# Attention and router kernel: the ranks of the tokens as two products of 16-bit whole numbers, 25 expert tiles without a branch, and one branch over all that remains

## The chip, the core and the metric

The kernel runs on one core of a Trainium2 chip. The metric is the time of one execution in microseconds of the device. The core has five engines that work side by side, each with its own queue of instructions: PE (TensorE, matrix products; the profile lists its loading of weights as PEld), DVE (VectorE), ACT (ScalarE), POOL (GpSimd, which here also issues the indirect DMAs) and SP (SyncE, which issues the other DMAs). They wait for each other with semaphores.

## What is computed

The reference has two parts. The first is attention with a block mask, for 4 batches, 8 heads, 768 positions and 64 values a head:

```python
scores = scale * np.matmul(q, k.transpose(0, 1, 3, 2))
scores = np.where(mask, scores, -1000000000.0)
attn = np.exp(scores - np.max(scores, axis=-1, keepdims=True))
attn = attn / (np.sum(attn, axis=-1, keepdims=True) + 1e-09)
attn_out = np.matmul(attn, v)
```

Its output, laid out as 3072 tokens of 512 values, goes to 8 experts. Each token takes one expert, the one whose embedding is nearest to it by cosine:

```python
logits = xn @ en.T / tau
expert_idx = np.argmax(logits, axis=1)
gate_w = probs[np.arange(N), expert_idx]      # softmax of the logits
for e in range(E):
    mask = expert_idx == e
    h = np.maximum(x[mask] @ w1[e], 0.0)      # 512 -> 1024
    out[mask] = gate_w[mask, None] * (h @ w2[e])   # 1024 -> 512
```

## The kernel before

**Attention** (`attention_fast`, up to about 320 us) runs over 16 pairs of heads. Each pair has 12 units of work: 128 keys against 384 queries, for two heads in 64x64 quarters of PE. For each unit PE makes the scores (L368), ACT the exponentials (L371), DVE adds up the denominators (L385, L387), and PE multiplies by v (L390). This path takes no maximum first; if a denominator comes out of bounds, a slow exact path (`exact`) has to compute everything again. `count_good` (L467 and after) counts the denominators that are in bounds into `good`.

**Routing** (`route`) follows each batch of 768 tokens: it makes the one-hot choice of each token, `oh`, on DVE (L541), and on POOL the running count `seen` of tokens by expert, one column of 128 tokens after another (L545, six small additions). **Ranks** (`rank`, L563 and after) then give each token its place among those with the same expert. Within a column of 128 tokens the number before a token is a product of a triangular matrix, `before`, with `oh` (L569). The number in earlier columns is a product of a matrix of ones with `seen` (L570), added up in the same place in PSUM. A third product with ones gives the totals by expert (L571), which DVE copies into `count` (L573). All are 32-bit. `rank` runs once a batch: three times amid attention, at a fixed unit of the plan in `after_sequence`, and the fourth time after the first expert tile, in `between` of `fast`.

**Experts.** Tokens are sorted by expert into tiles of 128. The first 5 tiles (`NE`) are made from the first two batches, while attention goes on; their places are computed by `dispatch_early`. All other tokens go into at least 19 late tiles (`NU`), because 24 x 128 = 3072, and at most 24 (`NL`), because an expert's last tile can be partly empty. How many are used is known on the device only, in `used` (L743), which `dispatch_late` computes on DVE. Two of the late tiles are mixed: they hold two experts, in halves of 64 tokens.

`expert_tiles` (L1087) runs the tiles. Each of them does the following.

- `fetch` (L850) issues on POOL the gathers of the rows of the tile after the next (L817, four indirect DMAs), and on SP the loads of the weights of up to three tiles ahead (L846, two loads of 2 MB for each expert).
- `expert_tile` (L886) makes the first layer on PE (L896, 64 products), takes its positive part on ACT (L899) and DVE (L903), and prepares the next tile's rows on DVE (L877 to L882). Then it makes the second layer (L911, 8 products of 512 columns, two passes each).
- `finish` multiplies by the gate on DVE (L919) and scatters the rows to the output by an indirect DMA on POOL (L920).

The first 24 tiles run always. The others stand in nested branches: the 25th runs if `used` is above 19, the 26th if it is above 20, and so on. Each branch is an instruction on each engine (L1105), which needs `used` in a register (L1104, a load). At the end of such a block each engine waits until all that was issued in it is done. The program is then at the last branch (L1204 and L1205), over the whole exact path, taken if `good` is not the full count. The instructions of the exact path stand between that branch and the end of the program.

The order of the instructions on an engine is that of the code, except where `issue_after` sets another; routing steps and ranks are put between units of attention by the plan in `after_sequence`.

## Time and profile before

Four runs took 698.47 to 699.81 us, with a median of 699.05. The profiled execution is another one:

| | us |
|---|---|
| profiled execution, time | 698.63 |
| profiled execution, span from the first to the last instruction | 696.8 |
| PE busy with matmuls | 682.0 |
| DVE busy | 344.9 |
| POOL busy | 296.4 |
| ACT busy | 188.4 |
| last matmul of PE ends at about | 683.9 |
| scatter of the last tile is issued by POOL at | 685.0 |

The profile's page gives the busy time of each engine, and the span in 40 equal slices, with the busy share of each engine in tenths and the clock that PE was granted. Other views list the waits of an engine with what ended them, the instructions of one line, or a stretch of time in order. In a row such as `L569 PE MATMUL rk<-oh,before` the line of the code comes first, then the engine, the operation and the names of the output and the inputs; `x8` is a count. An engine name with a q (POOLq) marks instructions that the engine's sequencer handles alone: branches, loads of registers, waits. PE's matmuls overlap, so a matmul's own duration is longer than the distance to the next one's start; distances between starts tell what PE needs for a piece of work.

### The profile page before, as it was taken

How to read it: one execution, taken by the hardware profiler on the slowest of the kernel's cores; microseconds unless marked ns; L12 is line 12 of the kernel's file. 1: busy time of each engine (PE TensorE's matmuls, PEld its weight loads, DVE VectorE, ACT ScalarE, POOL GpSimd, SP SyncE). 2: the span in 40 equal slices, each digit the busy share in tenths (PEclk: the TensorE clock that was granted, in tenths of full speed). 3: DMA queues.
4: the chain of work that ended last, by engine and by line, in shares of the span. 5: the costliest groups of instructions: out<-in, count | busy, mean ns of one | idle time of the engine just before them, and what ended most of it. 6: DMA issues, size and time to landing. Idle time of an engine off the chain costs nothing.

```text
span 696.8 us, 19415 instructions
## 1 busy us (share of the span) xinstructions
PE 682.0 (98%) x8237; PEld 452.9 (65%) x8237; DVE 344.9 (49%) x733; ACT 188.4 (27%) x266; POOL 296.4 (43%) x450
## 2 busy tenths in 40 slices
PE   9999999999999999999999999999999999999992
PEld 4777777555555557557767677666576755667770
DVE  6887778877788888765771111211112111211120
ACT  5455555555555455453100000000100000000000
POOL 1355466544774468545402244224332343323430
PEclk9999999999999999999999999999999999999997
DMA  7832344575326669653999889999899998999990
GB/s 122 132 68 51 47 70 71 130 155 108 59 42 155 141 160 210 218 162 106 330 407 375 324 313 343 341 348 320 305 409 403 406 370 310 420 391 418 353 346 25
DMA packets 172650, 164.87 MB, mean 237 GB/s; under 512 B 129340, under 2 KB 129340, under 8 KB 169478
## 3 DMA queue, kind: packets, MB, share of 16 engines
q1 hardware_dynamic: 165734, 149.86, 68.0%
q0 software_dynamic: 5216, 13.43, 5.2%
q8 instruction: 68, 1.11, 0.7%
q10 hardware_dynamic: 1600, 0.20, 0.2%
q14 instruction: 32, 0.26, 0.1%
HBM read 147.66 MB, written 16.07 MB: 235 GB/s over the span
## 4 chain that ended last, share of the span: by engine, by line
PE 96%; DMA 1%; issue 1%; POOL 0%; DVE 0%; ACT 0%; POOLq 0%
PE hp L896 23%; PE sc L368 22%; PE yp L911 22%; PE av L390 18%; PE back L425 3%; PE hp L939 2%; PE yp L959 2%; PE back L418 2%; DMA out_dram<-y,slot_l 1%; PE warm L81 1%; PE hp L951 0%; PE xg_ps L872 0%; PE rk L569 0%; POOL out_dram L920 0%; POOL xg L817 0%
## 5 line engine op out<-in xcount | busy, mean ns | idle before, releaser
L371 ACT ACTIVATE e<-sc 128x768 f32<-128x768 f32 x192 | 155.5, 810 | 149.1 <-PE sc L368 147.8
L896 PEld LDWEIGHTS hp<-xgt,w 128*128 128x128 f32 x1472 | 167.8, 192 | 10.8 <-issue 10.2
L896 PE MATMUL hp<-xgt,w 128*128 128x128 f32 x1472 | 169.3, 275 | 0.0
L368 PE MATMUL sc<-qt,kt 64*64 64x384 f32 x1536 | 163.5, 482 | 0.0
L911 PE MATMUL yp<-w,h 128*128 128x512 f32 x368 | 161.7, 592 | 0.0
L390 PE MATMUL av<-e,vld 64*64 64x384 f32 x1536 | 159.7, 486 | 0.0
L387 DVE TENSOR_TENSOR esum<-esum,e 128x768 f32<-128x768 f32 x128 | 129.2, 1010 | 34.2 <-ACT e L371 30.3
L911 PEld LDWEIGHTS yp<-w,h 128*128 128x128 f32 x368 | 68.2, 190 | 77.0 <-issue 76.0
L453 POOL TENSOR_TENSOR sq<-sq 128x192 f32<-128x192 f32 (+1 forms) x186 | 103.4, 556 | 13.9
L817 POOL DMA_INDIRECT xg<-x_dram,quarter x88 | 88.3, 1003 | 32.9 <-issue 27.7
L390 PEld LDWEIGHTS av<-e,vld 64*64 64x64 f32 x1536 | 63.7, 133 | 46.1 <-issue 17.3
L899 ACT ACTIVATE h<-hp 128x512 f32<-128x512 f32 x23 | 13.7, 597 | 291.4 <-PE hp L896 264.6
L903 DVE TENSOR_SCALAR h<-hp 128x512 f32<-128x512 f32 x23 | 15.9, 692 | 149.7 <-PE hp L896 146.3
L920 POOL DMA_INDIRECT out_dram<-y,slot_l x20 | 20.1, 1007 | 156.4 <-DVE y L919 151.1
L368 PEld LDWEIGHTS sc<-qt,kt 64*64 64x64 f32 x1536 | 66.2, 133 | 31.5 <-issue 22.8
L449 POOL TENSOR_TENSOR sq<-x 128x384 f32<-128x384 f32 x31 | 28.4, 917 | 115.6 <-DVE part L438 97.6
L368 PE MATMUL sc<-qmask,kmask 64*64 64x384 bf16 x768 | 72.6, 323 | 0.1
L919 DVE TENSOR_SCALAR y<-yp,gate 128x512 f32<-128x512 f32 x20 | 15.0, 751 | 81.0 <-PE yp L911 68.8
L368 PEld LDWEIGHTS <-kmask 64*64 64x64 bf16 x768 | 31.3, 107 | 26.4 <-issue 21.3
L385 DVE TENSOR_TENSOR esum<-e 128x768 f32<-128x768 f32 x32 | 31.2, 976 | 7.2 <-ACT e L371 7.1
L425 PE MATMUL back<-ones,esum 64*64 64x1 f32 x1536 | 27.5, 190 | 0.0
L425 PEld LDWEIGHTS back<-ones,esum 64*64 64x64 f32 x1536 | 26.6, 135 | 0.0
(204 smaller groups left out, 365.9 us busy)
## 6 DMA issues: line engine op xcount, KB each, us to landing
w<-in_moe_w_dram SPq DMA_DIRECT2D x54, 2048.0 KB
w<-in_moe_w_dram SPq DMA_DIRECT2D x16, 512.0 KB
x_dram<-x SPq DMA_DIRECT2D x24, 258.0 KB
vld<-in_v_dram SPq DMA_DIRECT2D x32, 192.0 KB
kld<-in_k_dram SPq DMA_DIRECT2D x60, 96.0 KB
qld<-in_q_dram SPq DMA_DIRECT2D x60, 96.0 KB
x_early<-x SPq DMA_DIRECT2D x12, 258.0 KB
xg<-x_dram,quarter POOLq DMA_INDIRECT x88
```

The costliest lines, as they stand in the source:

```text
L368: nc.tensor.matmul(ps[D * r:D * (r + 1), h, 0:HALF], lhsT=rows[D * h:D * (h + 1), keys], rhs=cols[D * h:D * (h + 1), queries], start=first ...
L371: k.exps = nc.scalar.activation(e, ps[:, :, 0:HALF], ACT.Exp, scale=SCALE)
L385: k.summed = nc.vector.tensor_tensor(out=k.esum, in0=k.first, in1=e, op=ALU.add)
L387: k.summed = nc.vector.tensor_tensor(out=k.esum, in0=k.esum, in1=e, op=ALU.add)
L390: nc.tensor.matmul(k.av[D * h:D * (h + 1), r, 0:HALF], lhsT=v[D * r:D * (r + 1), h, kc, :], rhs=e[D * r:D * (r + 1), h, :], start=(kc == 0 ...
L425: nc.tensor.matmul(sums[D * s:D * (s + 1), t, h, r:r + 1], lhsT=esum[D * r:D * (r + 1), h, cols], rhs=k.ones[D * r:D * (r + 1), 0:1], star ...
L449: nc.gpsimd.tensor_tensor(out=sq, in0=x, in1=x, op=ALU.mult)
L453: k.squared = nc.gpsimd.tensor_tensor(out=out, in0=sq[:, :, 0:width], in1=sq[:, :, width:2 * width], op=ALU.add).ins
L817: k.nc.gpsimd.indirect_dma_start(out=x[:, g], out_offset=None, in_=quarters, in_offset=bass.IndirectOffsetOnAxis(ap=k.quarter[:, g, t:t + ...
L896: nc.tensor.matmul(hp[:, f, :], lhsT=w1[:, d, (f0 + f) * P:(f0 + f + 1) * P], rhs=xt[:, d, :], start=(d == 0), stop=(d == ND - 1))
L911: nc.tensor.matmul(yp, lhsT=h[:, f, :], rhs=w2[:, f, :], start=(f == 0), stop=(f == NF - 1))
L920: k.scattered = nc.gpsimd.indirect_dma_start(out=k.out[:, :], out_offset=bass.IndirectOffsetOnAxis(ap=slot, axis=0), in_=y[:, :], in_offse ...
```

## The change

The ranks. `oh`, `seen`, the triangular matrix and a second matrix of ones become 16-bit (bf16, in which whole numbers up to 256 are exact). The product with ones now spans the seven columns of `seen` at once, the six for the ranks and the one for the totals, and comes first; the product with `before` is added to six of them. So two products take the place of three.

The tiles. `FULL = min(NU + 1, NL)` is 20. The 5 + 20 = 25 tiles always run, in one loop, and `fetch` and `prepare` look no further than the last of them (`k.stop`). Before, they looked ahead to all 29 tiles that there could be.

The branch. `count_good` also computes `todo`: one if a denominator was out of bounds, plus one if `used` is above 20. A single branch on `todo` stands behind the loop. In it, `more` runs the tiles from the 26th on, in nested branches on `used` as before, but with their own buffers and without any loads ahead, and then the branch on `good` with the exact path.

```diff
+FULL = min(NU + 1, NL)
...
-    k.before = pool.tile([P, P], F32, name="before")
+    k.ones_b = pool.tile([P, P], BF16, name="ones_b")
+    nc.vector.memset(k.ones_b, 1.0)
+    k.before = pool.tile([P, P], BF16, name="before")
...
-    k.oh = pool.tile([P, NT, E], F32, name="oh")
+    k.oh = pool.tile([P, NT, E], BF16, name="oh")
     k.rank = pool.tile([P, NT], F32, name="rank")
-    k.seen = pool.tile([P, NT + 1, E], F32, name="seen")
+    k.seen = pool.tile([P, NT + 1, E], BF16, name="seen")
...
+    bad = k.dp.tile([P, 1], F32, name="bad")
+    nc.vector.tensor_scalar(out=bad, in0=ps[:, 0:1], scalar1=float(N * H), scalar2=None, op0=ALU.is_lt)
+    tiles = k.dp.tile([P, 1], F32, name="tiles")
+    nc.vector.tensor_scalar(out=tiles, in0=k.used, scalar1=float(FULL), scalar2=None, op0=ALU.is_gt)
+    k.todo = k.const.tile([P, 1], I32, name="todo")
+    nc.vector.tensor_tensor(out=k.todo, in0=bad, in1=tiles, op=ALU.add)
...
-    nc.tensor.matmul(rk, lhsT=k.before, rhs=oh, start=True, stop=False)
-    nc.tensor.matmul(rk, lhsT=k.ones, rhs=k.seen[:, b * NC:(b + 1) * NC, :], start=False, stop=True)
-    nc.tensor.matmul(ps[:, NC * E:(NC + 1) * E], lhsT=k.ones, rhs=k.seen[:, (b + 1) * NC, :], start=True, stop=True)
+
+    nc.tensor.matmul(ps[:, 0:(NC + 1) * E].rearrange("p (c e) -> p c e", e=E), lhsT=k.ones_b,
+                     rhs=k.seen[:, b * NC:(b + 1) * NC + 1, :], start=True, stop=False)
+    nc.tensor.matmul(rk, lhsT=k.before, rhs=oh, start=False, stop=True)
...
-    if i + 2 < NE + NL and i + 2 != NE:
+    if i + 2 < k.stop and i + 2 != NE:
         fetch_rows(k, i + 2)
-    need = [(t, at) for t in range(NE + NL) for at in parts(t)]
+    need = [(t, at) for t in range(k.stop) for at in parts(t)]
...
-    if i + 1 < NE + NL:
+    if i + 1 < k.stop:
         prepare(k, i + 1)
...
-    between, n.scattered = iter(between), None
-    for i in range(NE + NU):
+    between, n.scattered, n.stop = iter(between), None, NE + FULL
+    for i in range(NE + FULL):
...
+def last_tiles(n):
+
     used = n.nc.values_load(n.used[0:1, 0:1], min_val=0, max_val=NL)
     with ExitStack() as more:
-        for i in range(NU, NL):
+        for i in range(FULL, NL):
             more.enter_context(n.tc.If(used > i))
-            n.scattered = None
-            fetch(n, NE + i)
+            n.scattered = n.relu = None
+            n.stop = NE + i + 1
+            fetch_rows(n, NE + i)
+            for at in parts(NE + i):
+                for _ in fetch_weights(n, NE + i, at):
+                    pass
+            prepare(n, NE + i)
             expert_tile(n, NE + i)
...
+def more(n):
+
+    n.rings, n.loads = {}, 0
+    with ExitStack() as ctx:
+        def pool(name, bufs, **kw):
+            return ctx.enter_context(n.tc.tile_pool(name=name, bufs=bufs, **kw))
+
+        n.wp, n.wp2 = pool("wp_l", 1), pool("wp2_l", 1)
+        n.eps, n.hps = pool("eps_l", 1, space=PSUM), pool("hps_l", 1, space=PSUM)
+        last_tiles(n)
+    good = n.nc.values_load(n.good[0:1, 0:1], min_val=0, max_val=N * H)
+    with n.tc.If(good < N * H):
+        exact(n)
...
     fast(n)
-    good = n.nc.values_load(n.good[0:1, 0:1], min_val=0, max_val=N * H)
-    with tc.If(good < N * H):
-        exact(n)
+    todo = n.nc.values_load(n.todo[0:1, 0:1], min_val=0, max_val=2)
+    with tc.If(todo > 0):
+        more(n)
```

## The prediction

> **What bounds the kernel.** I read the page's first two parts, then the list of waits of TensorE (PE), then the stretches in which the change works, in order of time.

> ```profile
> span 696.8 us, 19415 instructions
> ...
> PE 682.0 (98%) x8237; PEld 452.9 (65%) x8237; DVE 344.9 (49%) x733; ACT 188.4 (27%) x266; POOL 296.4 (43%) x450
> ...
> PEclk9999999999999999999999999999999999999997
> ```

> ```profile
> PE warm L81 <- DVE zeros L78: 1.3, 1, 1.3
> PE hp L951 <- issue: 0.5, 2, 0.2
> ```

> PE is busy for 98% of the span at the full granted clock, and these two rows are all the waits that it has. No load of weights, gather or eviction holds it anywhere. So a microsecond taken out of PE's own work is a microsecond of the end, wherever it stands; the other part of the span to be had is the tail, from PE's last matmul (about 683.9 us) to 696.8 us: 12.9 us in which no engine computes for long. The change touches both.

> **The ranks.** They run four times: at 118.9, 198.2 and 278.1 us amid attention and at 340.1 us between the first two expert tiles. The timeline of PE shows the first and the last of them (start, busy us, line), and the nearest thing to what replaces them, a product with 16-bit weights of 128x128 and 10 columns, also amid attention:

> ```profile
> 118.95 0.42 PE L569 MATMUL rk<-oh,before 128*128 128x48 f32 x2
> 119.20 0.39 PE L570 MATMUL rk<-seen,ones 128*128 128x48 f32 x2
> 119.43 0.35 PE L571 MATMUL rk<-seen,ones 128*128 128x8 f32 x2
> 119.71 0.88 PE L390 MATMUL av<-e,vld 64*64 64x384 f32 x8
> ```

> ```profile
> 257.91 0.46 PE L658 MATMUL slot_ps<-val,lanes 128*128 128x10 bf16 x12
> 258.30 0.88 PE L390 MATMUL av<-e,vld 64*64 64x384 f32 x8
> ```

> ```profile
> 340.14 0.32 PE L569 MATMUL rk<-oh,before 128*128 128x48 f32 x2
> 340.30 0.39 PE L570 MATMUL rk<-seen,ones 128*128 128x48 f32 x2
> 340.52 0.35 PE L571 MATMUL rk<-seen,ones 128*128 128x8 f32 x2
> 340.73 1.47 PE L896 MATMUL hp<-xgt,w 128*128 128x128 f32 x11
> ```

> Each 32-bit product is two passes of weights and matmul, so a rank is six passes. From its first to the next work: 119.71 - 118.95 = 0.76 us in attention, 340.73 - 340.14 = 0.59 us among the tiles. The twelve 16-bit passes take 258.30 - 257.91 = 0.39 us, and their starts in the trace lie 26 ns apart, so two of them take 0.39 - 10 x 0.026 = 0.13 us, the switch back to the 64x64 matmuls included. Among the tiles the same line (24 passes at 369.71, the next matmul at 370.32) costs 25 ns a pass, two 0.05 us. The gain is 3 x (0.76 - 0.13) + (0.59 - 0.05) = 1.9 + 0.5 = **2.4 us**. Bounds: if each 16-bit product cost as much as a 32-bit one, one product of three goes, 0.22 us four times, 0.9 us; if the 0.08 us more that the first and third rank wait before they start went too, 2.6 us. I take 2.4, by the nearest row, which has the same weights, type and neighbours.

> What stands around it: the product with the counts now comes first, so PE waits for GpSimd's adds (L545) 0.2 us sooner. At the first rank they end at 112.94 + 2.93 = 115.87 us, 3.1 us ahead; at the last at 340.07 us, 0.07 us before PE is free. I cost this at 0 to 0.1 us. VectorE gets a fill of the 16-bit ones and three tiny operations (0.16 us each by their neighbours, 0.5 in all). The nearest matmul to need VectorE behind them is the fifth yp of the first tile after the rank, due at 348.39 + 4 x 0.43 = 350.1 us; its half of h is ready at 348.85. The 1.2 us between hide it, so nothing; without that cover it would be 0.5 us. New waits of PE on itself (the first `back` after a rank, the first slot_ps) are for matmuls a score group or more earlier, and cost nothing; draining PE there, 0.5 us by the length of one sc matmul, four times 2 us, would be the other end, and stays inside the range.

> **The 25th tile.** Line 920 scatters 5 + 20 tiles, so the 25th tile runs in this data already, behind the branch. PE has no gap at that branch (14.0 us between the starts of tiles, as before it), because its sequencer runs ahead: PE's own branch row stands at 665.8 us, the matmuls behind it start at 669.7. So running it always saves nothing in PE. Four weight loads of 2 MB (SP, at 650 to 670 us) and eight gathers of 1.0 us on GpSimd, made for tiles 26 and 27, go; nothing waits for them, and they cost nothing either way.

> **The tail.** Here the branches matter. Rows of the branch lines, with the times of first and last start:

> ```profile
> L1104 POOLq TENSOR_LOAD <-used x1: 516/516/516, 670.7 to 670.7; - x1
> ```

> ```profile
> L1105 POOLq EVENT_SEMAPHORE  x4: 17/43/43, 685.0 to 688.6; - x4
> ```

> ```profile
> L1205 POOLq EVENT_SEMAPHORE  x6: 17/30/43, 692.3 to 692.8; - x6
> ...
> L1205 POOLq COMPARE_BRANCH  x1: 50/50/50, 689.6 to 689.6; - x1
> L1205 POOLq INC_SWDGE_SEM  x1: 410/410/410, 694.5 to 694.5; - x1
> ```

> The last y ends at 684.71 us. GpSimd issues its scatter (684.99 to 686.00), waits at the join of the inner branches until it has landed (688.4), releases its queue (688.7, 0.42), loads `good` (689.3, 0.30) and branches over the fallback at 689.6. Its next instruction starts at 692.3, 2.7 us later; in between only instruction packets move. VectorE shows the same at its own jump (685.4 to 688.3). Then come waits to 692.8, 1.7 us with nothing, the queue's release at 694.5, a drain, and the end.

> After the change there is one branch and no join ahead of it. GpSimd loads `todo` as soon as the last scatter is handed over. The load of `used` shows when that is: y of the tile before ended at 670.70, the load began at 670.7, beside the scatter (670.98), and the branch ran at 671.3. So: y ends 684.71, branch 685.3, jump 2.7, first instruction behind it at 688.0 instead of 692.3. The scatter lands at 688.4 meanwhile, when the waits reach it. From there to the end all stays: **4.3 us** less. PE and VectorE jump no later than today and are done by 689.0, so GpSimd still ends last. Bounds: 0.7 us, if the load is held until the scatter has landed (3.6 us later than I take it); 5.9 us, if the idle 1.7 us before the release goes as well. I take 4.3, from the same engine's own load and jump.

> [...]

> **The sum.** 2.4 + 4.3 = 6.7 us. The profiled execution took 698.63 us (span 696.8), so 691.9 by it; the median of the four runs, 699.05, lies 0.4 above, so **692.3 us**.

> **Rivals.**
> - *The second pause goes too* (0.20). The 1.7 us before the last release look like a second piece of code that is fetched because the jump lands near the end of the first. The new code lies elsewhere. SP shows such a second pause (677.6 to 681.4), VectorE and ACT, which have less left to run, do not. 2.4 + 5.9 = 8.3 us: 690.8.
> - *The jump is not moved forward* (0.10). GpSimd's load of `todo` waits for the scatter, or the fetch takes as long as SP's (671.5 to 677.6, 6.1 us). For it: the old join did wait for the landing. Against it: the load of `used` did not. 2.4 + 0.7 = 3.1: 696.0.
> - *Slower* (0.04): GpSimd's adds of 16-bit counts. They take 0.20 us, but 0.85 to 0.89 for the first and last of each group in attention, so they can be slow. With x us more for each, the last rank waits 6x - 0.07 and the other three 6x - 3.1 each. The whole gain is gone at 24x - 9.4 = 6.7, x = 0.67; at x = 0.8 it is 4.7 + 3 x 1.7 = 9.8 us, 702.1. Against it: as many elements, half the bytes, no other operation.
> - *It does not do what it says* (0.04): 16-bit products at the price of 32-bit ones and the tail as before, 698.1.

> **Numbers.** The forecast has 0.62. Low end: 2.6 + 5.9 from 699.05 and 0.4 for the spread of the runs, 690.1. High end: a rank gain of 0.9 and a tail gain of 3.1 (load 1 us later, after the scatter's issue, and a jump of 2.9), 695.1. Left out are the second, third and fourth rival, 0.18. About 0.2%, 1.4 us, is what a measurement of this kernel can tell from no change. Faster: 0.62 + 0.20 + 0.10 = 0.92; same 0.04; slower 0.04.

> **What would show it.** Right: `rk` on PE as two 16-bit matmuls, 0.13 us to the next av; PE's last matmul at about 681.5; GpSimd's branch 0.6 us after the last y and its next instruction 2.7 us later; in short, a tail of about 8.6 us behind PE where it is 12.9 now. Wrong: a wait of PE at `rk` for L545, a gap at `back` or slot_ps, or GpSimd's load of `todo` starting after the landing.

## The result and the profile after

The change made the kernel slightly slower. The median is 700.28 us over 40 runs (699.78 to 701.06), beside 699.25 for the kernel before over 60 runs next to them. The ratio is 1.0017 with a 95% interval of 1.0012 to 1.0021, which is about 1.2 us. The profiled execution has a span of 698.6 us, where it was 696.8.

The page's first lines, and the list of PE's waits, of the kernel after:

```profile
span 698.6 us, 19311 instructions
...
PE 679.3 (97%) x8221; PEld 427.1 (61%) x8221; DVE 343.3 (49%) x734; ACT 188.4 (27%) x266; POOL 289.3 (41%) x442
...
PEclk9999999999999999999999999999999999999995
```

```profile
PE warm L82 <- DVE zeros L79: 1.3, 1, 1.3
PE sc L371 <- DVE qt L288: 0.5, 1, 0.5
PE hp L962 <- issue: 0.5, 2, 0.2
```

PE does 2.7 us less work in 16 matmuls fewer, and its one new wait, 0.5 us, stands at the very start. The change did to PE what it was meant to, and yet the span grew. The time is therefore lost behind PE. The timeline of PE at the first rank and at the last (start, busy us, line) confirms the first half of this:

```profile
119.08 0.20 PE L580 MATMUL rk<-seen,ones_b 128*128 128x56 bf16 x1
119.12 0.18 PE L582 MATMUL rk<-oh,before 128*128 128x48 bf16 x1
119.23 0.88 PE L393 MATMUL av<-e,vld 64*64 64x384 f32 x8
```

```profile
338.37 0.19 PE L580 MATMUL rk<-seen,ones_b 128*128 128x56 bf16 x1
338.40 0.18 PE L582 MATMUL rk<-oh,before 128*128 128x48 bf16 x1
338.42 0.80 PE L907 MATMUL hp<-xgt,w 128*128 128x128 f32 x5
```

From the first product to the next work it is now 119.23 - 119.08 = 0.15 us amid attention, and 0.05 us among the tiles. The last rows of PE's timeline, before the change and after it:

```profile
677.75 6.17 PE L911 MATMUL yp<-w,h 128*128 128x512 f32 x14
```

```profile
677.59 4.03 PE L922 MATMUL yp<-w,h 128*128 128x512 f32 x9
```

PE now ends at 677.59 + 4.03 = 681.6 us, where it was 677.75 + 6.17 = 683.9. Behind it come 16.9 us to the end of the span, where it was 12.9.

Now the tail. These are the rows of POOL's load of `todo`, of its branch over `more` and of its queue's release (count, shortest/median/longest ns, first and last start):

```profile
L1240 POOLq TENSOR_LOAD <-todo x1: 503/503/503, 682.4 to 682.4; - x1
```

```profile
L1241 POOLq EVENT_SEMAPHORE  x6: 17/30/43, 685.7 to 686.2; - x6
...
L1241 POOLq COMPARE_BRANCH  x1: 53/53/53, 683.0 to 683.0; - x1
L1241 POOLq INC_SWDGE_SEM  x1: 2388/2388/2388, 686.2 to 686.2; - x1
```

The last y ends at 682.4 us. POOL loads `todo` at once, branches 0.6 us later, and has its next instruction 2.7 us after that. The release of the queue, INC_SWDGE_SEM, begins at 686.24 us, where it began at 694.47: POOL is 8.2 us ahead of before. The next two rows are the program's last drain on POOL, first before the change, then after it:

```profile
L1234 POOLq DRAIN  x3: 46/107/1055, 694.9 to 696.5; - x3
```

```profile
L1270 POOLq DRAIN  x3: 40/107/9061, 688.7 to 698.3; - x3
```

The longest of the three drains took 1.055 us and takes 9.061. The release took 0.410 us and takes 2.388. Together that is 8.01 + 1.98 = 10.0 us given back, 1.8 more than the 8.2 that had been won. In these 9 us no engine computes. The last scatter's packets landed at 685.1 us, and SP, the last of the other engines, is through with its waits by 689.4.

What is different about POOL's queue? In the trace of before POOL issues 118 indirect DMAs, in that of after 110. The eight that are missing are the gathers ahead for tiles 26 and 27. And in before POOL's timeline shows an idle at the 114th of them, ended by no other engine, that is nowhere else as long (the last column in brackets is the idle time before it, and what ended it):

```profile
670.98 1.01 POOL L920 DMA_INDIRECT out_dram<-y,slot_l  x1 [7.78 <-DVE y L919]
674.72 1.03 POOL L817 DMA_INDIRECT xg<-x_dram,quarter  x1 [2.73 <-issue]
676.05 1.00 POOL L817 DMA_INDIRECT xg<-x_dram,quarter  x1 [0.30 <-issue]
```

The gather at 674.72 us is the 114th. It comes 2.7 us behind the scatter, where a gather usually follows in 0.3.

**The theory** from these rows: POOL's queue keeps an entry for every indirect DMA, and keeps it after the transfer is done. Only when the queue is full, at the 114th of these DMAs, are the finished ones taken back, which cost 2.4 us in before beside PE's work. A kernel that never fills the queue takes all of them back at its end, in the last drain, at 9.06 / 110 = 0.08 us each. The change went from the one side of this line to the other. **Rivals:** the drain is long because POOL issued nothing but scatters in its last 36 us (the idle theory); or because the block that the branch skips is larger, whatever the number of DMAs (the block theory); or a drain has a fixed price if nothing was taken back before.

### The profile page after: what moved, and what is told of

It is laid out like the page before. It is cut to its first block, busy times and chain, and to the rows that moved or that the text cites. A ratio compares the mean times of both kernels' runs of the same rounds, so it can differ in the third digit from the quotient of the medians.

```text
span 698.6 us, 19311 instructions
## 1 busy us (share of the span) xinstructions
PE 679.3 (97%) x8221; PEld 427.1 (61%) x8221; DVE 343.3 (49%) x734; ACT 188.4 (27%) x266; POOL 289.3 (41%) x442
## 4 chain that ended last, share of the span: by engine, by line
PE 96%; DMA 1%; DVE 0%; issue 0%; ACT 0%; POOL 0%; POOLq 0%
PE hp L907 24%; PE yp L922 23%; PE sc L371 22%; PE av L393 18%; PE back L428 3%; PE hp L950 2%; PE yp L970 2%; PE back L421 2%; DMA kld<-in_k_dram 0%; PE hp L962 0%; DMA qld<-in_q_dram 0%; PE xg_ps L883 0%; PE slot_ps L669 0%; ACT e L374 0%; PE quarter_ps L686 0%
## 5 line engine op out<-in xcount | busy, mean ns | idle before, releaser
L371 PE MATMUL sc<-qt,kt 64*64 64x384 f32 x1536 | 158.0, 482 | 0.5 <-DVE qt L288 0.5
L393 PE MATMUL av<-e,vld 64*64 64x384 f32 x1536 | 154.2, 486 | 0.0
L390 DVE TENSOR_TENSOR esum<-esum,e 128x768 f32<-128x768 f32 x128 | 128.2, 1001 | 32.6 <-ACT e L374 29.4
L828 POOL DMA_INDIRECT xg<-x_dram,quarter x80 | 80.3, 1003 | 28.1 <-issue 23.2
L393 PEld LDWEIGHTS av<-e,vld 64*64 64x64 f32 x1536 | 55.1, 133 | 53.5 <-issue 26.3
L371 PEld LDWEIGHTS sc<-qt,kt 64*64 64x64 f32 x1536 | 58.8, 133 | 39.2 <-issue 36.2
L452 POOL TENSOR_TENSOR sq<-x 128x384 f32<-128x384 f32 x31 | 30.7, 992 | 112.5 <-DVE part L441 96.6
L371 PE MATMUL sc<-qmask,kmask 64*64 64x384 bf16 x768 | 65.9, 323 | 0.1
L371 PEld LDWEIGHTS <-kmask 64*64 64x64 bf16 x768 | 24.7, 107 | 33.0 <-issue 33.0
```

Source lines behind the costliest of these rows:

```text
L371: nc.tensor.matmul(ps[D * r:D * (r + 1), h, 0:HALF], lhsT=rows[D * h:D * (h + 1), keys], rhs=cols[D * h:D * (h + 1), queries], start=first ...
L390: k.summed = nc.vector.tensor_tensor(out=k.esum, in0=k.esum, in1=e, op=ALU.add)
L393: nc.tensor.matmul(k.av[D * h:D * (h + 1), r, 0:HALF], lhsT=v[D * r:D * (r + 1), h, kc, :], rhs=e[D * r:D * (r + 1), h, :], start=(kc == 0 ...
L452: nc.gpsimd.tensor_tensor(out=sq, in0=x, in1=x, op=ALU.mult)
L828: k.nc.gpsimd.indirect_dma_start(out=x[:, g], out_offset=None, in_=quarters, in_offset=bass.IndirectOffsetOnAxis(ap=k.quarter[:, g, t:t + ...
```

## The experiments

### One part of the change alone

The first kernel is before with the change of the ranks, of which the diff shows the main lines; the second is after with the ranks of before.

```diff
-    k.seen = pool.tile([P, NT + 1, E], F32, name="seen")
+    k.seen = pool.tile([P, NT + 1, E], BF16, name="seen")
...
-    nc.tensor.matmul(rk, lhsT=k.before, rhs=oh, start=True, stop=False)
-    nc.tensor.matmul(rk, lhsT=k.ones, rhs=k.seen[:, b * NC:(b + 1) * NC, :], start=False, stop=True)
-    nc.tensor.matmul(ps[:, NC * E:(NC + 1) * E], lhsT=k.ones, rhs=k.seen[:, (b + 1) * NC, :], start=True, stop=True)
+    nc.tensor.matmul(ps[:, 0:(NC + 1) * E].rearrange("p (c e) -> p c e", e=E), lhsT=k.ones_b,
+                     rhs=k.seen[:, b * NC:(b + 1) * NC + 1, :], start=True, stop=False)
+    nc.tensor.matmul(rk, lhsT=k.before, rhs=oh, start=False, stop=True)
```

The ranks alone:

> The kernel before with the change of the ranks alone; tiles, branches and all 118 indirect DMAs stay. Every theory: the ranks bring what the profile after shows, PE's last matmul about 2.3 us earlier, and the tail of before (12.9 us) stays, since nothing is taken from POOL's queue: about 699.05 - 2.3 = 696.8 us. If instead the ranks are what lost the time, the tail behind PE grows with this alone, to 17 us as after the change, and the time is about 700.

Measured: 696.38 us, ratio 0.9959 (0.9946 to 0.9973), that is 2.9 us less, between 1.9 and 3.8. POOL's last drain stays short:

```profile
L1236 POOLq DRAIN  x3: 46/107/1055, 692.4 to 694.0; - x3
```

The 25 tiles and the one branch alone:

> After with the ranks of before (three 32-bit products): the part with the 25 tiles and the one branch alone, 110 indirect DMAs. Queue theory: the end of after, behind a PE that is done 2.3 to 2.8 us later: 700.3 + 2.3 to 2.8 = 702.6 to 703.1 us, last drain 9.06. If the two parts worked upon each other (the long drain comes only with the 16-bit ranks), about 693.

Measured: 703.04 us, ratio 1.0057 (1.0043 to 1.0070), 4.0 us more. The drain:

```profile
L1268 POOLq DRAIN  x3: 40/107/9061, 691.4 to 701.1; - x3
```

The two parts simply add: -2.9 + 4.0 = +1.1, and the whole change measures +1.2. The ranks gain; the other part loses more. What it loses is in this drain and in the release, which takes 2.388 us here too.

### Three gathers more, and four

Both are after with a few gathers more, at tile 23, into a buffer of their own that nothing reads. Only their number differs; the diff has the kernel with four.

```diff
+SPARE, SPARE_AT = 4, {23: 4}
...
+def spare_rows(k, i, n):
+
+    if not hasattr(k, "spare"):
+        k.spare = k.wp.tile([P, SPARE, XE], F32, name="spare")
+        k.spared = 0
+    quarters = k.x_dram.rearrange("n (e w) -> (n e) w", e=ND)
+    with k.tc.issue_after(k.scattered):
+        for _ in range(n):
+            k.nc.gpsimd.indirect_dma_start(
+                out=k.spare[:, k.spared % SPARE], out_offset=None, in_=quarters,
+                in_offset=bass.IndirectOffsetOnAxis(ap=k.quarter[:, k.spared % NG, 0:1], axis=0),
+                bounds_check=quarters.shape[0] - 1, oob_is_err=False,
+            )
+            k.spared += 1
...
 def fetch(k, i):
+    if not k.exact and i in SPARE_AT:
+        spare_rows(k, i, SPARE_AT[i])
```

With 3, so 113 in all:

> After, plus 3 gathers of 128 rows into a buffer of their own that nothing reads, issued at tile 23: 113 indirect DMAs in all. Queue theory (POOL's software queue keeps an entry for each of its DMAs until the 114th forces it to take them back; if that never happens, the last drain walks all of them): no 114th, so the last drain of POOL stays at about 113 x 0.082 = 9.3 us and the release at 2.4; about 700.5. Idle theory (the drain is long because POOL issued no DMA but the scatters for its last 36 us): the drain falls to about 1 us, 690 to 691. Block theory (the long drain belongs to the larger block that is skipped, whatever the number of DMAs): as after, 700.3.

With 4, so 114:

> As the one with 3, but 4 such gathers: 114 indirect DMAs. Queue theory: the 114th, the last scatter or one shortly before it, has a pause of about 2.4 us ahead of it in which the entries are taken back, and the last drain falls to about 1 us and the release to 0.4; if the pause falls on the last scatter it costs up to 2.4 us of the end, so about 690 to 693. Idle theory: the same as with 3, 690 to 691. Block theory: as after, 700.3.

Measured: 700.44 us with 113 (ratio to before 1.0019, 1.0010 to 1.0029) and 691.86 with 114 (0.9892, 0.9877 to 0.9907). One gather more makes the kernel 8.6 us faster. The last drains, with 113 first:

```profile
L1290 POOLq DRAIN  x3: 40/107/9306, 688.4 to 698.2; - x3
```

```profile
L1290 POOLq DRAIN  x3: 40/107/731, 688.5 to 689.8; - x3
```

The kernel with 113 rules out the idle theory: it has gathers just as late as the one with 114, and its drain is long. The kernel with 114 rules out the block theory: it skips the same block, and its drain is short. The pause moved too. POOL's timeline of the kernel with 114, with its last scatter, the 114th, and its load of `todo`:

```profile
668.82 1.01 POOL L951 DMA_INDIRECT out_dram<-y,slot_l  x1 [7.77 <-DVE y L950]
684.30 1.00 POOL L951 DMA_INDIRECT out_dram<-y,slot_l  x1 [14.47 <-issue]
```

```profile
L1260 POOLq TENSOR_LOAD <-todo x1: 504/504/504, 684.1 to 684.1; - x1
```

Here y was ready at 682.5 us, but POOL's load of `todo`, which comes with the scatter, starts at 684.09. These 1.5 us of the taking back are on the path that sets the end. Where that DMA stands earlier, they should be hidden, and the next kernel places it there.

### Eight gathers more, early

As above, with 4 gathers at tile 8 and 4 at tile 9.

```diff
+SPARE, SPARE_AT = 4, {8: 4, 9: 4}
```

> After, plus 8 such gathers, but early, 4 at tile 8 and 4 at tile 9: 118 indirect DMAs as before, none added in the last 200 us. Queue theory: the 114th is a gather or scatter of the last tiles but two, its pause of 2.4 us lies beside PE's work, the last drain is about 1 us and the release 0.4: about 10 us less than after, 690.2. Idle theory and block theory: nothing is different at the end, the drain stays at 9 us, 700.3.

Measured: 693.47 us, ratio 0.9923 (0.9909 to 0.9936). The drain is as the queue theory has it, though nothing was added in the last 200 us, which speaks once more against the idle theory. The time is 3.3 us above what I expected, and PE's waits have a new first row:

```profile
L1290 POOLq DRAIN  x3: 40/107/1057, 689.7 to 691.3; - x3
```

```profile
PE yp L942 <- issue: 2.5, 2, 1.3
```

The two waits, from 450.4 and 466.0 us, fall where POOL issues eight gathers on end in place of four. There PE waits for the half of h that DVE makes. These are the rows of the first wait, and DVE's row at the same tile in the kernel after:

```profile
450.93 0.69 DVE L934 TENSOR_SCALAR h<-hp 128x512 f32<-128x512 f32 x1 [10.28 <-remote]
451.68 1.55 PE L942 MATMUL yp<-w,h 128*128 128x512 f32 x3 [1.23 <-issue]
```

```profile
448.36 0.69 DVE L914 TENSOR_SCALAR h<-hp 128x512 f32<-128x512 f32 x1 [7.58 <-PE hp L907]
```

DVE starts 3.9 us after PE's last product of the first layer ended (447.01), where in the kernel after it starts 1.2 us after that product (447.14); PE's signal, for which DVE waits, is in the trace at 450.91 and 448.34 us. Why it comes late stays open. Gathers alone do not decide it: the experiments ran on three chips, and in the two on the third (the 25 tiles alone, and the one with 16 rows) DVE starts 0.04 us behind at all tiles with four gathers. In any case, gathers that nothing reads are not free everywhere. The pause ahead of the 114th is only 0.48 us here, 0.2 above the usual:

```profile
647.65 1.01 POOL L829 DMA_INDIRECT xg<-x_dram,quarter  x1 [0.48 <-issue]
```

So the taking back has no fixed price: 0.2, 1.5, 1.8 and 2.4 us were seen. Why it differs stays open.

### The eight gathers ahead, issued again

The plainest test of the step that the prediction took: after, with the look-ahead of the gathers as long as before. The four weight loads for these tiles stay out, so they cannot be what is regained.

```diff
+AHEAD = 2
...
-    if i + 2 < k.stop and i + 2 != NE:
+    if i + 2 < k.stop + AHEAD and i + 2 != NE:
         fetch_rows(k, i + 2)
```

> After, but the eight gathers ahead for tiles 26 and 27, which the change removed, are issued again as before (nothing reads them): 118 indirect DMAs; one branch, ranks and weight loads as after. Queue theory: the 114th, a gather of the last block of four, takes the entries back beside PE's work, the last release is 0.43 us and the last drain 1.06 as with the 8 early gathers (12 entries left); POOL's load of todo at 682.45 us as after, 6.42 us from there to the end as there, and 1.7 outside the span: 690.6 us. If the eight gathers cost nothing either way, as the prediction said: 700.3.

Measured: 690.23 us, ratio 0.9867 (0.9850 to 0.9883), which is 8.2 to 10.5 us less than before. POOL's release and its last drain:

```profile
L1242 POOLq INC_SWDGE_SEM  x1: 428/428/428, 686.2 to 686.2; - x1
```

```profile
L1271 POOLq DRAIN  x3: 40/107/1057, 686.6 to 688.2; - x3
```

The release begins at 686.2 us as after the change, and from there all is as before the change: 8.3 us less in the span, 688.5 where it was 696.8. Its timeline has the pause at the 114th, beside PE's work:

```profile
668.42 1.01 POOL L932 DMA_INDIRECT out_dram<-y,slot_l  x1 [7.75 <-DVE y L931]
671.51 1.03 POOL L829 DMA_INDIRECT xg<-x_dram,quarter  x1 [2.08 <-issue]
```

Eight gathers that nobody reads are worth 10 us. No other version here is faster.

### Before, without these gathers

The same step in the kernel before.

```diff
-    if i + 2 < NE + NL and i + 2 != NE:
+    if i + 2 < NE + NU + 1 and i + 2 != NE:
         fetch_rows(k, i + 2)
...
             n.scattered = None
+            if i > NU:
+                fetch_rows(n, NE + i)
             fetch(n, NE + i)
+            if i > NU:
+                n.relu = None
+                prepare(n, NE + i)
             expert_tile(n, NE + i)
```

> Before, with 32-bit ranks and its branches, without the eight gathers ahead for tiles 26 and 27 (tiles behind the branches gather their own rows): 110 indirect DMAs. Queue theory: the kernel before gets the same end as after: last drain 9.06 instead of 1.06 us, release 2.4 instead of 0.4 (once or twice): 709 to 711 us. If the long drain belongs to the one larger branch of after: as before, 699.2.

Measured: 709.77 us, ratio 1.0147 (1.0130 to 1.0164). The releases at its two joins, and the last drain:

```profile
L1105 POOLq INC_SWDGE_SEM  x1: 2379/2379/2379, 689.0 to 689.0; - x1
```

```profile
L1210 POOLq INC_SWDGE_SEM  x1: 2357/2357/2357, 695.1 to 695.1; - x1
```

```profile
L1239 POOLq DRAIN  x3: 46/107/9056, 697.5 to 707.2; - x3
```

So the kernel before owed its short tail to work that it never used. The release is slow at both joins, and the drain behind them is long all the same, which shows that a release takes nothing back.

### A drain in an idle stretch

After, with its 110 DMAs and one drain on POOL behind the scatter of tile 22.

```diff
 def fetch(k, i):
+    if i == NE + FULL - 2 and not k.exact:
+        with k.tc.issue_after(k.scattered):
+            k.nc.gpsimd.drain()
```

> After with its 110 indirect DMAs, plus one drain on POOL behind the scatter of tile 22, where POOL has been idle for some 12 us at a time. Queue theory: this drain takes some 9 us there, beside PE's work, and takes back 108 entries; the release is 0.3 us and the last drain 0.2 to 0.7 for the few that are left, so about 690 us. If the number of DMAs since the start decides, or the block that is skipped, the last drain stays at 9 us and the time at 700.3 or above.

Measured: 690.54 us, ratio 0.9873 (0.9856 to 0.9889). The drain that was added, and the last one:

```profile
L865 POOLq DRAIN  x1: 10147/10147/10147, 654.4 to 654.4; - x1
```

```profile
L1274 POOLq DRAIN  x3: 46/107/222, 686.5 to 688.3; - x3
```

The drain takes the entries back, as the short release and last drain show. It starts at 654.44 us, and the scatter ahead of it is issued until 655.68; the other 8.9 us are the cost as it was seen at the end, only paid where POOL has nothing to do. The last drain is 0.84 us shorter than with the eight gathers, and yet the time is no better: 1.05 us without any instruction follow it, until 687.77 us. With the eight gathers the instruction behind the drain starts at 687.73. Something else, 2.1 us behind the first instruction after the jump, is late then; the prediction took such a pause in before for the fetch of a second piece of code. In that pause of before, from 692.8 to 694.5 us, one instruction packet moved, from 692.96 us for 0.44 us; whether POOL waits for it, no run tested.

### Fewer DMAs, and smaller ones

Fewer first: after without the gathers of tiles 13 to 24; the kernel leaves these rows out and computes the tiles from the rows of earlier ones.

```diff
+SKIP = 13
...
+        if SKIP <= i < NE + FULL and not k.exact:
+            pass
-        if late:
+        elif late:
```

> After without the gathers of tiles 13 to 24: 62 indirect DMAs. (This part of the computation is left out: those tiles are computed from the rows of earlier tiles.) Queue theory, by the slopes of the runs so far, 0.0817 us an entry for the drain (9.306 for 113, 9.061 for 110) and 0.02 for the release: drain 0.08 + 62 x 0.0817 = 5.1 us, release 0.19 + 62 x 0.02 = 1.4, so 4.9 us less than after, about 695.4. A fixed price of a drain without an earlier taking back: 9 us as after, 700.3.

Measured: 695.53 us, ratio 0.9941 (0.9925 to 0.9958); the release takes 1.428 us. The drain:

```profile
L1273 POOLq DRAIN  x3: 40/107/5141, 688.2 to 693.9; - x3
```

No fixed price, then. Last, the kernel with four late gathers, each of 16 rows in place of 128:

```diff
-                out=k.spare[:, k.spared % SPARE], out_offset=None, in_=quarters,
-                in_offset=bass.IndirectOffsetOnAxis(ap=k.quarter[:, k.spared % NG, 0:1], axis=0),
+                out=k.spare[0:16, k.spared % SPARE], out_offset=None, in_=quarters,
+                in_offset=bass.IndirectOffsetOnAxis(ap=k.quarter[0:16, k.spared % NG, 0:1], axis=0),
```

> As the one with 4 late gathers (114 indirect DMAs, 691.9 us), but each of the four fetches 16 rows instead of 128. If the queue counts DMAs, the 114th takes the entries back as there: last drain 0.7 us, about 691.9. If it counts rows or descriptors, the four small ones do not fill it: no taking back, last drain about 9.1 to 9.4 us, 700.4.

Measured: 700.75 us, ratio 1.0026 (1.0017 to 1.0035):

```profile
L1290 POOLq DRAIN  x3: 46/107/9382, 689.2 to 699.2; - x3
```

There are 114 DMAs again, but nothing was taken back. What fills the queue is therefore not the number of DMAs but what they consist of. It is not their bytes either: with eight gathers early the queue was found full after 12.2 MB had moved on it, and in the kernel with 113 DMAs 13.1 MB did not fill it. Of number, bytes and rows that leaves the rows: 128 in each of these, 16 in the four small ones. The price of the drain, on the other hand, goes by their number: the four small ones cost as much as large ones. All the lengths of the last drain lie on one line, 0.075 us + 0.0817 us for each DMA that was not yet taken back:

| kernel | DMAs | last drain, us | DMAs not taken back, by the line | release, us |
|---|---|---|---|---|
| a drain behind tile 22 | 110 | 0.222 | 1.8 | 0.235 |
| four late gathers | 114 | 0.731 | 8 | 0.348 |
| eight gathers ahead, issued again | 118 | 1.057 | 12 | 0.428 |
| without the gathers of tiles 13 to 24 | 62 | 5.141 | 62 | 1.428 |
| after | 110 | 9.061 | 110 | 2.388 |
| three late gathers | 113 | 9.306 | 113 | 2.448 |
| four late gathers of 16 rows | 114 | 9.382 | 114 | 2.468 |

The line is drawn through 62 and 110. Its confirmation is that it gives 113 and 114 where so many were issued, 8 and 12 in two kernels of which one issues four DMAs more, and about 2 behind the drain of tile 22, where two were issued (0.24 us by the line, 0.222 measured). The release follows 0.19 us + 0.02 us for each in the same way.

## Why the prediction was wrong

- *The ranks* were right. I forecast 0.13 us amid attention and 0.05 among the tiles, and 2.4 us in all. The trace has 0.15 and 0.05, PE is done 2.3 us sooner, and alone they bring 2.9 us (1.9 to 3.8).
- *PE* gains nothing from running the 25th tile always: right. No wait at `rk`, `back` or slot_ps came.
- *The branch and the jump* were right to a tenth of a microsecond: load of `todo` with the end of y, branch 0.6 us later, 2.7 us to the next instruction. The second pause, the 1.7 us ahead of the release, went as well, which I had as the first rival. POOL stood at the release 8.2 us ahead of before, and 8.3 was that rival's sum. So the forecast's own term for the tail up to there, 4.3, was too small; it measured 8.2 - 2.3 = 5.9 us. With the eight gathers issued again the time is 690.2, beside the 690.8 of that rival.
- *What failed* is one sentence: eight gathers for tiles 26 and 27 go, "nothing waits for them, and they cost nothing either way". From it came the next, "From there to the end all stays". Nothing waited for the gathers' data, that was true. But the 114th DMA, one that serves a tile which never runs here, was what had the queue taken back. Without it the release and the drain cost 1.98 + 8.01 = 10.0 us at the end, where no engine has work to hide them. The sum of -8.2 and +10.0 is the 1.8 us by which the span of the profiled execution grew.
- *The rivals.* None of them named the queue, so the loss came through a door that I had not looked at. Two rows of before could have pointed to it: the one idle of 2.7 us ahead of the 114th DMA, and a drain of 1.06 us, which I let stand as a constant. I had read the drain as the end of the program, not as work that depends on what came before it.

## What to carry to other kernels

A DMA that nothing reads is not always free to remove (with eight of them this kernel runs in 690.2 us, without in 700.3): count what it shares with the others, its queue's entries among that, and look for what the queue does when it fills and when the program ends. Where a kernel issues many indirect DMAs on GpSimd, see to it that their entries are taken back while GpSimd is idle, by filling the queue a little before the end or by a drain of one's own behind an early scatter; two versions of this kernel that do so run in 690.2 and 690.5 us. And a change that gains at one place and loses at another shows little in the total: the rows of the tail, one instruction after the other, showed both.
